# Weight guards issued ahead of the copies of h, w_out's tiles in another order, and other times for loads and spills

## The chip, the core and the metric

One core of a Trainium2 chip runs the whole kernel in one launch. The metric is the device time of an execution in microseconds. The engines are named TensorE (PE in the profile, its weight loads PEld), VectorE (DVE), ScalarE (ACT), GpSimd (POOL) and SyncE (SP, which issues nearly all DMAs).

## The reference

A retention layer without softmax feeds a two-layer network. Per batch entry b (8) and head (8), over 576 positions with 64 channels:

```python
scores = scale * np.matmul(q, k.transpose(0, 1, 3, 2))
Dmat = np.where(rel >= 0, gamma[:, None, None] ** rel[None, :, :], 0.0)
attn = np.matmul(scores * Dmat[None], v)
x = attn.transpose(0, 2, 1, 3).reshape(B * S, H * D)      # 4608 x 512
h = x @ w_in                                              # 512 x 2048
out = (h - np.tanh(h)) @ w_out                            # 2048 x 512
```

All arrays are float32 but the two weight matrices, which come as 64-bit floats.

## The kernel before

**Tiling.** The 576 positions are cut into 9 chunks of 64. A chunk with all 8 batch entries is one block of 512 tokens, and the network runs block by block: `mm1(n, f)` makes tile f (of 16) of h for block n, 12 matmuls of 128x128 by 128x512; `mm2(n, f)` multiplies tile f of h - tanh(h) by w_out's tile f into four output tiles, also 12 matmuls. Each operand is held as a high and a low word, and three products are summed. The retention runs chunk by chunk with a carried state; `entry(p)` handles pair p of batch entries: the output of pair p, the scores of pair p + 1 and the state update, interleaved on TensorE. VectorE then multiplies the scores by a mask into `pm` (L263), ScalarE and VectorE make the two words of x (L278, L280).

**Weights.** w_in and w_out come in 16 tiles each, numbered 0 to 31 in the order `stream` (w_in's 0 to 15, then w_out's in the order `turn`). A tile is loaded raw (`load_w`, 512 KB), and a unit of conversion turns it into two words in the same place: a *guard* on ScalarE (L95 tanh and L98 abs, which make a mask in a buffer of the tag `cv`), three instructions on VectorE (L105, L110, L112), the high word on ScalarE (L117), and the low word on VectorE (L124), which is issued by the next unit's first step. `step()` advances a unit by a third.

**The order of work.** Every engine follows the order in which the program issues its instructions. The first loop over `seq` has 32 iterations, k = 0 to 31: `mm1(0, f)` for k below 16, then `mm1(1, f)`, with entries 4 to 7 after k = 5, 8, 10 and 14. An iteration does one step, `mm1`, then two more steps (one from k = 24 on, none for the last two iterations). Unit u = k + 2 is converted in iteration k. ScalarE's order in an iteration is: copy of h(k) out of its PSUM bank, guard of unit u + 1, high word of unit u; the guard sits in the unit's second step, after mm1. Four banks take h in turn. Then come the loads: `upto("load", k + 7)` issues all tiles with an index below k + 7 (k + 6 from k = 11 on), and `behind` makes each wait for the latest copy of h.

**Places and spills.** h of block 0 and 1 can't be used before w_out is there. Most copies go to memory at once (`g`, spilled by SyncE at L341). Ten tiles of block 0 first stay in places of w_out's tiles (`home`) and are spilled later, place 7, 13, 12, 11 and 10 at k = 16 to 20. Other places of w_out hold early data too: pairs 6 and 7 in 0 to 3, the first chunk's keys in 4 and 5, a table in 6, the first chunk's inputs in 8 to 15. Pair 16 is loaded in halves at k = 9 and 10, pair 17 at k = 14; GpSimd scales their v (L186), and pair 17's q (L185).

**After the loop**, a loop over `late` fetches the spilled tiles one by one (`fetch`), takes tanh and difference (`resume`, L368 and L369), splits them (`words`, L375 and L376) and runs mm2 on them; what is left of the units is done in its first iterations. Blocks 2 to 8 follow with mm1 and mm2 in alternation.

Of the kernel before, what the change touches and what calls it, by code (L numbers as in the profile page):

```python
# [9 lines left out]
F32 = mybir.dt.float32  # L10
F32R = mybir.dt.float32r
I32 = mybir.dt.int32
BF16 = mybir.dt.bfloat16
AF = mybir.ActivationFunctionType
ALU = mybir.AluOpType
PSUM = bass.MemoryType.PSUM

B, H, S, D = 8, 8, 576, 64
NT, DM, DF = B * S, H * D, 2048
P = 128  # L20
NF = DF // P
NCC = DM // P
C = 64
NC = S // C
BLK = B * C
# [33 lines left out]
def behind(tc, name):  # L59

    tc.add_manual_dep(
        tc.nc.cur_bb.bb.instructions[-1], name,
        mybir.DependencyInfo(mybir.DependencyClass.Sync, mybir.DependencyReason.DATA), reason="paced",
    )
# [3 lines left out]
def retention_ffn(ctx: ExitStack, tc: tile.TileContext, ins, out, spill):  # L68
# [4 lines left out]
    pool = ctx.enter_context(tc.tile_pool(name="pool", bufs=2))  # L73
# [3 lines left out]
    mask = const.tile([P, C], F32, name="mask")  # L77
# [3 lines left out]
    win, wout, wraw, masks = {}, {}, {}, {}  # L81
# [9 lines left out]
    def guard(t, f, begin=False):  # L91

        if (t, f) not in masks:
            masks[t, f] = pool.tile([P, DM], I32, tag="cv", bufs=3, name=f"m{t}{f}")
            nc.scalar.activation(masks[t, f], wraw[t, f][:, :, 1].bitcast(F32), AF.Tanh, scale=STEP)  # L95
            if begin:
                return
        nc.scalar.activation(masks[t, f], masks[t, f], AF.Abs, scale=HI_BITS)  # L98

    def unit(k):  # L100

        t, f = stream[k]
        hw, lw = wraw[t, f][:, :, 1], wraw[t, f][:, :, 0]
        z = masks.pop((t, f))
        nc.vector.scalar_tensor_tensor(z, hw, 3, z, op0=ALU.logical_shift_left, op1=ALU.bitwise_and)  # L105
        finish()
        yield
        if 0 < k and k + 1 < at_["load"]:
            upto("guard", k + 2)
        nc.vector.scalar_tensor_tensor(z, lw, 29, z, op0=ALU.logical_shift_right, op1=ALU.bitwise_or)  # L110
        yield
        nc.vector.scalar_tensor_tensor(z, hw, -0x40000000, z, op0=ALU.bitwise_and, op1=ALU.bitwise_or)  # L112
        if k == 0:
            yield
        del wraw[t, f]
        w = const.tile([P, 2, DM], F32R, tag=f"w{t}{f}", name=f"w{t}{f}")
        nc.scalar.copy(w[:, 0], z.bitcast(F32))  # L117
        (wout if t == "o" else win)[f] = w if t == "o" else w.rearrange("p s (c m) -> p s c m", m=P)
        last.append((w, z))

    def finish():
        while last:
            w, z = last.pop()
            nc.vector.tensor_tensor(w[:, 1], z.bitcast(F32), w[:, 0].bitcast(F32), op=ALU.subtract)  # L124


    turn = [NF - 2, NF - 1] + list(range(NF - 2))
    stream = [("i", f) for f in range(NF)] + [("o", f) for f in turn]
    at_ = {"load": 0, "guard": 0, "convert": 0}
    last, going, pace = [], [], []  # L130

    def upto(what, n):
        while at_[what] < min(n, 2 * NF):
            {"load": load_w, "guard": guard}[what](*stream[at_[what]])
            at_[what] += 1
# [17 lines left out]
    loaded, scored, xs, qtabs = {}, {}, {}, {}  # L153

    def load_qtab(c):
        if c not in qtabs:
            if c == 1:
                qtabs[c] = const.tile([P, 4, C], F32, tag="wo6", name="qtab1")
            else:
                qtabs[c] = pool.tile([P, 4, C], F32, tag="qtab", bufs=1, name=f"qtab{c}")  # L160
            nc.sync.dma_start(qtabs[c], qtab_d[c - 1])

    def load_pair(p, u=None):

        if p >= NP:
            return
        c, pr = divmod(p, B // 2)
        load_qtab(c)
        a = loaded["pair", p] if u == 1 else pool.tile([P, 2, 4, 4, C], F32, tag="a", name=f"a{p}")
        if u is None:  # L170
            nc.sync.dma_start(a, qkv_d[c - 1, 2 * pr : 2 * pr + 2].rearrange("u p t i s -> p u t i s"))
        else:
            nc.sync.dma_start(a[:, u], qkv_d[c - 1, 2 * pr + u])
        loaded[2 * p], loaded[2 * p + 1] = a[:, 0], a[:, 1]
        loaded["pair", p] = a
        loaded["qv", p] = a[:, :, 0], a[:, :, 2]

    def prep(p, q=True):
        if p >= NP:
# [12 lines left out]
    def load_early(p):  # L192
        c, pr = divmod(p, B // 2)
        if pr < 2:
            return load_pair(p)
        src = qkv_d[c - 1, 2 * pr : 2 * pr + 2].rearrange("u p t i s -> p u t i s")
        parts = []
        for t in range(2):
            parts.append(const.tile([P, 2, 2, 4, C], F32, tag=f"wo{2 * (pr - 2) + t}", name=f"a_early{p}_{t}"))
            nc.sync.dma_start(parts[t], src[:, :, 2 * t : 2 * t + 2])  # L200
            behind(tc, pace[-1])
        for u in range(2):
            loaded[2 * p + u] = Parts([part[:, u] for part in parts])
        loaded["qv", p] = parts[0][:, :, 0], parts[1][:, :, 0]

    def scale_q(p):
        q, table = loaded["qv", p][0], qtabs[p // (B // 2)]
# [7 lines left out]
    def half(k):  # L215
        return slice(64 * k, 64 * k + 64)
# [38 lines left out]
    def after_score(j, sc, n):  # L255

        if j < B:

            pm = pool.tile([P, 2, 4, C], F32, tag="gh", name=f"pm{j}")
            nc.vector.tensor_tensor(pm[:, 0], sc[:, 0], decay, op=ALU.mult)  # L260
        else:
            pm = pool.tile([P, 2, 4, C], F32, tag="pm", bufs=1, name=f"pm{j}")
            nc.vector.tensor_tensor(  # L263
                pm[:, :n].rearrange("p u i q -> p (u i) q"), sc.rearrange("p u i q -> p (u i) q"),
                mask.unsqueeze(1).broadcast_to([P, 4 * n, C]), op=ALU.mult,
            )
        for u in range(n):
            scored[j + u] = pm[:, u]
# [49 lines left out]
    home = {0: 7, 1: 7, 6: 13, 7: 13, 8: 12, 9: 12, 11: 11, 12: 11, 13: 10, 14: 10}  # L318
# [45 lines left out]

    def resume(n, f):
        g = fetched[n, f]
        th = pool.tile([P, BLK], F32, tag="cv", bufs=3, name=f"th{n}_{f}")
        nc.scalar.activation(th, g, AF.Tanh)  # L368
        nc.vector.tensor_tensor(g, g, th, op=ALU.subtract)  # L369

# [29 lines left out]
    def store(n, t):  # L400
        o = ops[n][t]
        if n == 1:

            if t == 0:
                obs[n] = pool.tile([P, 4, DM], F32, tag="xl", name=f"ob{n}")
            ob = obs[n][:, t]
        else:
            ob = pool.tile([P, DM], F32, tag="cv", bufs=3, name=f"ob{n}_{t}")
        if t % 2 == 0:
            nc.scalar.copy(ob, o)  # L410
        else:
            nc.vector.tensor_copy(ob, o)  # L412
        for u in range(2):
            nc.sync.dma_start(out[2 * t + u, n * C : (n + 1) * C], ob[half(u)])
# [110 lines left out]
    seq = [(n, f) for n in range(2) for f in range(NF)]  # L525
    late = [(1, f) for f in turn] + [(0, f) for f in range(NF)]
    early = {5: 4, 8: 5, 10: 6, 14: 7}
    scales = {2: 4, 4: 5, 7: 6, 9: 7, 13: 8}
    for k, (n, f) in enumerate(seq):
        last_two = k - (len(seq) - 2)  # L530
        if k in (2, 7):
            scale_k(k // 4)
        if k + 1 in early:
            scale_v(early[k + 1])
        if last_two < 0:
            step()
        else:
            fetch(*late[2 + last_two])
        mm1(n, f, ("h", "o2", "h", "o3")[k % 4] if k < len(seq) - 4 else ("o2", "o3", "h", "h")[k % 4])
        if last_two < 0:  # L540
            step()
            if k < 24:
                step()
        if k in scales:
            scale_q(scales[k])
        upto("load", k + (7 if k < 11 else 6))
        if k in (2, 5):
            load_early(B // 2 + 2 + (k - 2) // 3)
        if k in (9, 10):
            load_pair(B, k - 9)  # L550
        for f in [f for f in home if home[f] == (7, 13, 12, 11, 10)[k - NF]] if NF <= k < NF + 5 else []:
            nc.sync.dma_start(spill[0, f], homes[home[f]][:, (f + 1) % 2 if f > 1 else f])
        if k == 3:
            nc.sync.dma_start(krows[1], krows_d[1])
            behind(tc, pace[-1])
            sc = scores_of(B // 2 - 1)
            ms, done = first_states(0, "new")
            run(m_score(B, sc[:, 0]) + m_score(B + 1, sc[:, 1]) + ms, [])
            after_score(B, sc, 2)
            done()  # L560
        if k in early:
            p = early[k]
            more = first_states(2 * (p - 3), f"o{(p + 1) % 2}") if p < B - 1 else None
            entry(p, scores_of(p), more)
        if k == 14:
            load_pair(B + 1)
        if k in (26, 28):
            prep(B + (k - 26) // 2, k == 28)
    p = B
# [16 lines left out]
    for n in range(2, NC):  # L586
        for f in range(NF):
            mm1(n, f)
            if n + 1 < NC and f % 4 == 1:

                sc = psp.tile([P, 2, 4, C], F32, tag="h", bufs=2, name=f"s{n}_{f}")
# [62 lines left out]
```

## Time and profile before

| what | value |
|---|---|
| three runs, median (lowest to highest) | 890.47 us (888.77 to 890.8) |
| profiled execution, its time | 891.8 us |
| profiled execution, its span | 890.0 us |
| mean granted TensorE clock | 0.995 |
| DMA moved | 82.06 MB |

The span runs from the first to the last instruction of the profiled execution; its time has 1.8 us more. All times below are microseconds from the start of the span. In a timeline the first number is the start, the second the length, and a bracket gives the idle time before the instruction and what ended it.

### The profile page before, as it was taken

The page shows a single profiled execution, that of the slowest core. Times are in us where ns is not written, and L with a number is a line of the kernel's source. Part 1 is how long each engine was busy: PE and PEld are TensorE (multiplying, and loading weights), DVE is VectorE, ACT ScalarE, POOL GpSimd, SP SyncE. Part 2 cuts the span into 40 slices and gives each one's busy share as a digit, 9 for nine tenths or more (in the row PEclk, how much of TensorE's full clock was granted, in tenths as well). Part 3 has the DMA queues.
Part 4 walks back from the last instruction along what each step waited for, and adds up shares of the span by engine and source line. Part 5 has one row for each costly group of instructions (what it writes and reads, how often), then busy time and mean ns, then how long its engine had stood idle before and what let it go on. Part 6 is the DMA issues. An engine that isn't in the chain of part 4 may idle for free.

```text
span 890.0 us, 17595 instructions
## 1 busy us (share of the span) xinstructions
PE 877.6 (99%) x7848; PEld 724.3 (81%) x7848; DVE 363.3 (41%) x548; ACT 287.7 (32%) x503; POOL 67.7 (8%) x59
## 2 busy tenths in 40 slices
PE   7999999999999999999999999999999999999997
PEld 6777878788888888888888888888888888888886
DVE  6879777653432332333233233323323322222222
ACT  4887774443222222222222222222222221222222
POOL 0001001210111110111111111111000111000000
PEclk8999999999999999999999999999999999999999
DMA  9966965551311131102111131113111201002001
GB/s 354 325 231 212 342 193 171 167 167 48 96 54 49 48 96 49 54 30 68 47 54 49 49 95 54 49 48 96 49 54 47 62 35 48 1 1 49 1 1 47
DMA packets 31372, 82.06 MB, mean 92 GB/s; under 512 B 3776, under 2 KB 4928, under 8 KB 31296
## 3 DMA queue, kind: packets, MB, share of 16 engines
q1 hardware_dynamic: 30768, 80.02, 27.8%
q8 instruction: 61, 1.00, 0.5%
q10 hardware_dynamic: 528, 0.92, 0.3%
q14 instruction: 15, 0.12, 0.0%
HBM read 63.62 MB, written 17.30 MB: 91 GB/s over the span
## 4 chain that ended last, share of the span: by engine, by line
PE 90%; DMA 3%; DVE 3%; ACT 2%; issue 0%; SPq 0%; DVEq 0%
PE o L393 44%; PE h L327 38%; PE s L252 3%; DMA rwo<-in_w_out_dram 2%; PE new L252 2%; PE own L252 2%; DMA rwi<-in_w_in_dram 1%; DVE mo L110 0%; DVE mo L112 0%; ACT mi L95 0%; ACT mi L98 0%; PE new_first L252 0%; DVE mi L105 0%; DVE wi L124 0%; ACT wi L117 0%
## 5 line engine op out<-in xcount | busy, mean ns | idle before, releaser
L327 PE MATMUL h<-xh,wi 128*128 128x512 f32 x1152 | 307.0, 392 | 2.7 <-ACT g L339 0.8
L393 PE MATMUL o<-wo,gh 128*128 128x512 f32 x1144 | 291.6, 393 | 0.4 <-DVE ob L412 0.4
L327 PEld LDWEIGHTS h<-xh,wi 128*128 128x128 f32 x1152 | 216.3, 189 | 49.7 <-ACT g L339 1.3
L393 PEld LDWEIGHTS o<-wo,gh 128*128 128x128 f32 x1144 | 212.3, 188 | 46.8 <-DVE ob L412 1.5
L354 DVE TENSOR_TENSOR g<-h,g 128x512 f32<-128x512 f32 x114 | 78.8, 691 | 367.1 <-ACT g L353 367.1
L353 ACT ACTIVATE g<-h 128x512 f32<-128x512 f32 x114 | 68.3, 599 | 420.9 <-PE h L327 420.1
L393 PE MATMUL o<-wo,gl 128*128 128x512 f32 x572 | 157.3, 389 | 0.0
L327 PE MATMUL h<-xl,wi 128*128 128x512 f32 x576 | 154.5, 390 | 0.0
L327 PEld LDWEIGHTS h<-xl,wi 128*128 128x128 f32 x576 | 108.7, 189 | 22.9
L393 PEld LDWEIGHTS o<-wo,gl 128*128 128x128 f32 x572 | 107.4, 188 | 22.3
L356 DVE TENSOR_TENSOR gl<-g,gh 128x512 fp32r<-128x512 f32 x113 | 81.0, 717 | 77.5 <-ACT gh L355 70.0
L355 ACT CAST gh<-g 128x512 fp32r<-128x512 f32 x113 | 70.1, 620 | 86.2 <-DVE g L354 86.2
L185 POOL TENSOR_TENSOR a<-a,qtab 128x512 f32<-128x512 f32 x27 | 36.3, 1344 | 605.7 <-DMA a<-in_qkv_dram 547.3
L252 PE MATMUL own<-a,state 64*64 64x64 f32 x960 | 58.9, 221 | 0.0
L252 PE MATMUL own<-pm,a 64*64 64x64 f32 x960 | 57.5, 218 | 0.0
L252 PEld LDWEIGHTS own<-a,state 64*64 64x64 f32 x960 | 47.8, 134 | 0.4 <-issue 0.4
L252 PEld LDWEIGHTS own<-pm,a 64*64 64x64 f32 x960 | 48.0, 135 | 0.0
L252 PEld LDWEIGHTS s<-a 64*64 64x64 f32 x960 | 30.3, 134 | 10.6 <-issue 10.2
L186 POOL TENSOR_TENSOR a<-a,vtab 128x512 f32<-128x512 f32 x28 | 32.2, 1152 | 67.4 <-DVE mi L112 67.4
L252 PE MATMUL s<-a 64*64 64x64 f32 x960 | 34.4, 221 | 0.0
L376 DVE TENSOR_TENSOR gl<-s,gh 128x512 fp32r<-128x512 f32 x30 | 21.6, 720 | 31.2 <-PE o L393 24.4
L375 ACT CAST gh<-s 128x512 fp32r<-128x512 f32 x30 | 18.6, 621 | 39.0 <-PE o L393 27.4
(67 smaller groups left out, 465.0 us busy)
## 6 DMA issues: line engine op xcount, KB each, us to landing
a<-in_qkv_dram SPq DMA_DIRECT2D x29, 1024.0 KB, 5.2
out_dram<-ob SPq DMA_DIRECT2D x69, 128.0 KB, 2.4
rwi<-in_w_in_dram SPq DMA_DIRECT2D x16, 512.0 KB, 5.8
rwo<-in_w_out_dram SPq DMA_DIRECT2D x16, 512.0 KB, 5.1
s<-spill_dram SPq DMA_DIRECT2D x30, 256.0 KB, 2.7
spill_dram<-g SPq DMA_DIRECT2D x20, 256.0 KB, 5.2
a<-in_first_dram SPq DMA_DIRECT2D x7, 384.0 KB, 5.0
spill_dram<-home SPq DMA_DIRECT2D x10, 256.0 KB, 6.3
```

The lines of the kernel that those rows point to most:

```text
L185: nc.gpsimd.tensor_tensor(a[:, :, 0], a[:, :, 0], table, op=ALU.mult)
L186: nc.gpsimd.tensor_tensor(a[:, :, 2], a[:, :, 2], vtab[:, c].unsqueeze(1).unsqueeze(3).broadcast_to([P, 2, 4, D]), op=ALU.mult)
L252: nc.tensor.matmul(out_, w, x, start=start, stop=stop)
L327: nc.tensor.matmul(hp, win[f][:, a, cc, :], x[:, cc, :], start=(k == 0), stop=(k == 3 * NCC - 1))
L353: nc.scalar.activation(g, h, AF.Tanh)
L354: nc.vector.tensor_tensor(g, h, g, op=ALU.subtract)
L355: nc.scalar.copy(gh, g)
L356: nc.vector.tensor_tensor(gl, g, gh.bitcast(F32), op=ALU.subtract)
L375: nc.scalar.copy(gh, g)
L376: nc.vector.tensor_tensor(gl, g, gh.bitcast(F32), op=ALU.subtract)
L393: nc.tensor.matmul(ops[n][t], g[:, t * P : (t + 1) * P], wout[f_][:, a, :], start=(f_ == first and k == 0), stop=(f_ == final and k == 2),)
```

## The change

Guards: a unit's first step now issues the guards of later units, up to unit u + 1 while u is below 5 and up to u + 2 from 5 on, as far as they are loaded; so ScalarE's order in an iteration becomes guard, copy of h(k), high word. The tag `cv` has four buffers instead of three; the room is taken from `pm`, which has no buffer any more: masked scores are written over the pair's k columns. `turn` becomes 14, 15, 8, 9, 4, 5, 6, 0, 1, 2, 3, 7, 13, 12, 11, 10. Loads follow a table `ahead` (as before up to k = 9, then 16, 18, 20, 21, 22, 23, and k + 8 from k = 16 on), home places are spilled at k = 12 (7), 13 (13), 14 (12), 16 (11) and 18 (10). Pair 16's second half is loaded at k = 11, pair 17 at k = 20; pair 7's q is scaled at k = 8 instead of 9 and the second half of the first chunk's keys at k = 6 instead of 7. The second step after mm1 stops at k = 22 instead of 24.

```diff
--- before.py
+++ after.py
@@ -91,7 +91,7 @@
     def guard(t, f, begin=False):
 
         if (t, f) not in masks:
-            masks[t, f] = pool.tile([P, DM], I32, tag="cv", bufs=3, name=f"m{t}{f}")
+            masks[t, f] = pool.tile([P, DM], I32, tag="cv", bufs=4, name=f"m{t}{f}")
             nc.scalar.activation(masks[t, f], wraw[t, f][:, :, 1].bitcast(F32), AF.Tanh, scale=STEP)
             if begin:
                 return
@@ -104,9 +104,12 @@
         z = masks.pop((t, f))
         nc.vector.scalar_tensor_tensor(z, hw, 3, z, op0=ALU.logical_shift_left, op1=ALU.bitwise_and)
         finish()
+        if k > 1:
+
+            upto("guard", min(k + (2 if k < 5 else 3), at_["load"]))
         yield
-        if 0 < k and k + 1 < at_["load"]:
-            upto("guard", k + 2)
+        if k == 1:
+            upto("guard", 3)
         nc.vector.scalar_tensor_tensor(z, lw, 29, z, op0=ALU.logical_shift_right, op1=ALU.bitwise_or)
         yield
         nc.vector.scalar_tensor_tensor(z, hw, -0x40000000, z, op0=ALU.bitwise_and, op1=ALU.bitwise_or)
@@ -124,7 +127,8 @@
             nc.vector.tensor_tensor(w[:, 1], z.bitcast(F32), w[:, 0].bitcast(F32), op=ALU.subtract)
 
 
-    turn = [NF - 2, NF - 1] + list(range(NF - 2))
+
+    turn = [14, 15, 8, 9, 4, 5, 6, 0, 1, 2, 3, 7, 13, 12, 11, 10]
     stream = [("i", f) for f in range(NF)] + [("o", f) for f in turn]
     at_ = {"load": 0, "guard": 0, "convert": 0}
     last, going, pace = [], [], []
@@ -173,7 +177,7 @@
             nc.sync.dma_start(a[:, u], qkv_d[c - 1, 2 * pr + u])
         loaded[2 * p], loaded[2 * p + 1] = a[:, 0], a[:, 1]
         loaded["pair", p] = a
-        loaded["qv", p] = a[:, :, 0], a[:, :, 2]
+        loaded["qk", p], loaded["qv", p] = a, (a[:, :, 0], a[:, :, 2])
 
     def prep(p, q=True):
         if p >= NP:
@@ -201,7 +205,7 @@
             behind(tc, pace[-1])
         for u in range(2):
             loaded[2 * p + u] = Parts([part[:, u] for part in parts])
-        loaded["qv", p] = parts[0][:, :, 0], parts[1][:, :, 0]
+        loaded["qk", p], loaded["qv", p] = parts[0], (parts[0][:, :, 0], parts[1][:, :, 0])
 
     def scale_q(p):
         q, table = loaded["qv", p][0], qtabs[p // (B // 2)]
@@ -259,10 +263,10 @@
             pm = pool.tile([P, 2, 4, C], F32, tag="gh", name=f"pm{j}")
             nc.vector.tensor_tensor(pm[:, 0], sc[:, 0], decay, op=ALU.mult)
         else:
-            pm = pool.tile([P, 2, 4, C], F32, tag="pm", bufs=1, name=f"pm{j}")
+
+            pm = loaded["qk", j // 2][:, :, 1]
             nc.vector.tensor_tensor(
-                pm[:, :n].rearrange("p u i q -> p (u i) q"), sc.rearrange("p u i q -> p (u i) q"),
-                mask.unsqueeze(1).broadcast_to([P, 4 * n, C]), op=ALU.mult,
+                pm, sc, mask.unsqueeze(1).unsqueeze(1).broadcast_to([P, 2, 4, C]), op=ALU.mult,
             )
         for u in range(n):
             scored[j + u] = pm[:, u]
@@ -364,7 +368,7 @@
 
     def resume(n, f):
         g = fetched[n, f]
-        th = pool.tile([P, BLK], F32, tag="cv", bufs=3, name=f"th{n}_{f}")
+        th = pool.tile([P, BLK], F32, tag="cv", bufs=4, name=f"th{n}_{f}")
         nc.scalar.activation(th, g, AF.Tanh)
         nc.vector.tensor_tensor(g, g, th, op=ALU.subtract)
 
@@ -405,7 +409,7 @@
                 obs[n] = pool.tile([P, 4, DM], F32, tag="xl", name=f"ob{n}")
             ob = obs[n][:, t]
         else:
-            ob = pool.tile([P, DM], F32, tag="cv", bufs=3, name=f"ob{n}_{t}")
+            ob = pool.tile([P, DM], F32, tag="cv", bufs=4, name=f"ob{n}_{t}")
         if t % 2 == 0:
             nc.scalar.copy(ob, o)
         else:
@@ -525,10 +529,13 @@
     seq = [(n, f) for n in range(2) for f in range(NF)]
     late = [(1, f) for f in turn] + [(0, f) for f in range(NF)]
     early = {5: 4, 8: 5, 10: 6, 14: 7}
-    scales = {2: 4, 4: 5, 7: 6, 9: 7, 13: 8}
+    scales = {2: 4, 4: 5, 7: 6, 8: 7, 13: 8}
+
+    ahead = {**{k: k + 7 for k in range(10)}, 10: 16, 11: 18, 12: 20, 13: 21, 14: 22, 15: 23}
+    leave = {12: 7, 13: 13, 14: 12, 16: 11, 18: 10}
     for k, (n, f) in enumerate(seq):
         last_two = k - (len(seq) - 2)
-        if k in (2, 7):
+        if k in (2, 6):
             scale_k(k // 4)
         if k + 1 in early:
             scale_v(early[k + 1])
@@ -539,16 +546,16 @@
         mm1(n, f, ("h", "o2", "h", "o3")[k % 4] if k < len(seq) - 4 else ("o2", "o3", "h", "h")[k % 4])
         if last_two < 0:
             step()
-            if k < 24:
+            if k < 22:
                 step()
         if k in scales:
             scale_q(scales[k])
-        upto("load", k + (7 if k < 11 else 6))
+        upto("load", ahead.get(k, k + 8))
         if k in (2, 5):
             load_early(B // 2 + 2 + (k - 2) // 3)
-        if k in (9, 10):
-            load_pair(B, k - 9)
-        for f in [f for f in home if home[f] == (7, 13, 12, 11, 10)[k - NF]] if NF <= k < NF + 5 else []:
+        if k in (9, 11):
+            load_pair(B, (k - 9) // 2)
+        for f in [f for f in home if home[f] == leave.get(k)]:
             nc.sync.dma_start(spill[0, f], homes[home[f]][:, (f + 1) % 2 if f > 1 else f])
         if k == 3:
             nc.sync.dma_start(krows[1], krows_d[1])
@@ -562,7 +569,7 @@
             p = early[k]
             more = first_states(2 * (p - 3), f"o{(p + 1) % 2}") if p < B - 1 else None
             entry(p, scores_of(p), more)
-        if k == 14:
+        if k == 20:
             load_pair(B + 1)
         if k in (26, 28):
             prep(B + (k - 26) // 2, k == 28)
```

## Rows read from the trace of the kernel before

**Rows 1.** The page: TensorE's busy time, and its busy tenths in 40 slices.
```profile
PE 877.6 (99%) x7848; PEld 724.3 (81%) x7848; DVE 363.3 (41%) x548; ACT 287.7 (32%) x503; POOL 67.7 (8%) x59
...
PE   7999999999999999999999999999999999999997
```

**Rows 2.** What TensorE waited for: total us, times, longest us.
```profile
PE s_first L252 <- DMA a<-in_first_dram: 2.8, 4, 1.4
...
PE s L252 <- ACT wi L117: 0.8, 1, 0.8
```

**Rows 3.** Windows: length, busy us of each engine, clock, DMA share, GB/s.
```profile
16.96:190.00 173.04, 169.95 (x1814) 138.80 (x1815) 134.17 (x202) 110.57 (x204) 13.32 (x9) 0.99 0.71 238
190.00:890.00 700.00, 695.30 (x5740) 575.44 (x5738) 220.71 (x327) 169.79 (x284) 54.14 (x46) 1.00 0.17 50
```

**Rows 4.** Timeline of TensorE around its stops.
```profile
44.48 1.20 PE L327 MATMUL h<-xh,wi 128*128 128x512 f32 x4 [0.80 <-issue]
...
58.19 1.19 PE L327 MATMUL h<-xh,wi 128*128 128x512 f32 x4
60.17 0.27 PE L252 MATMUL s<-a_early 64*64 64x64 f32 x2 [0.78 <-ACT wi L117]
...
72.03 0.96 PE L327 MATMUL h<-xh,wi 128*128 128x512 f32 x3 [0.43 <-ACT wi L117]
...
111.60 1.07 PE L327 MATMUL h<-xh,wi 128*128 128x512 f32 x4
113.52 1.20 PE L327 MATMUL h<-xh,wi 128*128 128x512 f32 x4 [0.85 <-ACT g L339]
...
130.05 2.11 PE L393 MATMUL o<-wo,gh 128*128 128x512 f32 x8
```

**Rows 5.** Timeline of VectorE.
```profile
59.38 0.68 DVE L208 TENSOR_TENSOR a_early<-a_early,qtab 128x512 f32<-128x512 f32 x1
...
68.04 1.35 DVE L105 SCALAR_TENSOR_TENSOR mi<-rwi,mi 128x512 int32<-128x512 int32 x1 [0.44 <-ACT mi L98]
...
127.42 0.68 DVE L369 TENSOR_TENSOR s<-s,th 128x512 f32<-128x512 f32 x1
128.03 0.69 DVE L105 SCALAR_TENSOR_TENSOR mo<-rwo,mo 128x512 int32<-128x512 int32 x1
```

**Rows 6.** Timeline of ScalarE.
```profile
38.05 0.58 ACT L339 COPY g<-h 128x512 f32<-128x512 f32 x1 [0.25 <-PE h L327]
...
45.01 0.59 ACT L333 COPY home<-h 128x512 f32<-128x512 f32 x1 [3.42 <-PE h L327]
...
66.18 0.59 ACT L333 COPY home<-h 128x512 f32<-128x512 f32 x1 [1.95 <-PE h L327]
66.66 0.68 ACT L95 ACTIVATE mi<-rwi 128x512 int32<-128x512 f32 x1
...
67.91 0.60 ACT L117 CAST wi<-mi 128x512 fp32r<-128x512 f32 x1
...
129.39 0.60 ACT L375 CAST gh<-s 128x512 fp32r<-128x512 f32 x1
```

**Rows 7.** An issue at 32.15; issues near 32, 73, 94, 61 us: us to landing.
```profile
32.15 0.59 SPq L86 DMA_DIRECT2D rwi<-in_w_in_dram  x1
...
rwi<-in_w_in_dram SPq DMA_DIRECT2D x1, 512.0 KB, 8.4
...
rwo<-in_w_out_dram SPq DMA_DIRECT2D x1, 512.0 KB, 3.5
...
rwo<-in_w_out_dram SPq DMA_DIRECT2D x1, 512.0 KB, 7.7
...
a<-in_qkv_dram SPq DMA_DIRECT2D x1, 512.0 KB, 6.1
```

**Rows 8.** Timeline of GpSimd.
```profile
67.80 1.04 POOL L186 TENSOR_TENSOR a<-a,vtab 128x512 f32<-128x512 f32 x1 [67.36 <-DVE mi L112]
```

**Rows 9.** What ScalarE waited for from 30 to 130 us: total us, times, longest us.
```profile
ACT mo L95 <- DMA rwo<-in_w_out_dram: 5.4, 5, 2.1
```

## The prediction

> **What bounds the kernel now.** I read the page first: TensorE is busy for nearly the whole span [rows 1], so time can only be won where it stands still. The list of what TensorE waited for has the first loads on top and then single waits, none that repeats [rows 2]. The windows then say where room is: up to 190 us its busy time falls 3.1 us short of the window, the DMA engines are 71% busy and VectorE and ScalarE are both loaded; from 190 us on the DMA share is 17% and the slices of the page show TensorE full but for the last one [rows 1, 3]. All that the diff touches runs before about 150 us, except where a masked score is kept, which I come to. So this is a question of a handful of stalls between iteration 6 and the start of the late loop, and the reader should see how small the stake is.
>
> **What each stall costs.** After a stop, four matmuls show 1.20 us and eight 2.11 [rows 4]: one more every (2.11 - 1.20) / 4 = 0.23 us. Four without a stop show 1.07. So the next group is due 4 x 0.23 = 0.91 after such a group starts, 0.16 before its shown end, and a stop costs its idle time + 0.16 + 0.13 for the slow restart, less when another kind of matmul follows. The stop at 113.52, idle 0.85, costs 1.1; at 72.03, idle 0.43, 0.7; at 60.17, idle 0.78, 0.85 (the attention block would have started 0.1 late anyway). The stop at 44.48, idle 0.80, has no releaser ("issue"), and I expect nothing of it. The three that the diff can reach are worth 1.1 + 0.7 + 0.85 = 2.65 us, 0.3% of the time. A 0.2% bound, 1.8 us, about what a measurement of this kernel can tell from no change, needs two thirds of that. What does the new order charge for them?
>
> **Entry(6), the wait at 60.17.** VectorE's scaling of pair 7's q (L208) ends at 60.06 [rows 5]; the timeline names ScalarE's high word of unit 11 [rows 4]. The first moves an iteration earlier (`scales` 9 to 8), the second loses the guard ahead of it (1.25 us on ScalarE, 66.66 to 67.91 [rows 6]). Gain 0.85, bounds 0 and 0.85; I take it whole.
>
> **Guards ahead of the copies of h: what they wait for.** ScalarE runs its program in order, so a guard placed ahead of the copy of h(k) holds that copy, and behind it the high word of unit k+2 that mm1(k+2) needs, until the guard's raw tile has landed. From unit 5 on the guard is for unit u+2 = k+4. The load table for k up to 9 is as before: iteration k issues index k+6, behind its copy of h. So the tile that iteration k+2 guards ahead of its copy was issued after copy k: the lead falls from about three copies to under two.
>
> The tightest case is index 9, issued at 32.15 and landed 8.4 us later, at 40.5, with the queue full [rows 7]; the spill and the load ahead of it keep that order, so it lands at 40.5 again even when issued a microsecond later. Before, its guard came after the copy at 45.01 and waited for nothing. Now it stands ahead of the copy of h(5), which began at 38.05 [rows 6]. From 40.5: guard 1.25, copy 0.5, then casting entry(4)'s output 1.1 (with unit 7's word), and on VectorE xl, state, L105, L124, L110, L112 at 0.6 to 0.7 each [rows 5], then unit 8's word 0.6: 40.5 + 1.25 + 0.5 + 1.1 + 6 x 0.64 + 0.6 = 47.8 with 0.1 of handovers. The matmul at 44.48 is the last of mm1(6), so mm1(8) is due at 44.48 + 0.23 + 12 x 0.227 = 47.4. Cost 0.45; bounds 0 (landing 0.5 earlier) and 2.3 (landing as late after its issue as before, 1.8 more).
>
> The second case is index 16, w_out's tile 14. `ahead[10]` is 16, so it moves from iteration 10 to 11, behind the copy of h(11), and iteration 12 guards it ahead of the copy of h(12). Before, mm1(14) restarted at 72.03; with 0.85 gone, a slow restart of 0.1 at 58.19 too [rows 4], and 0.45 added, copy 11 moves from 66.18 to about 65.7, and with the 0.6 gone mm1(14) would be due at 70.9. The load is issued at 66.25, when that copy ends. One such load took 3.5 us where nothing else moved and 7.7 in the saturated stretch, a half pair with a load ahead of it 6.1 [rows 7]; here the queue is empty, so I take 4.2, near the first. Landing 70.4, guard 1.25, copy 0.5, word 0.6 and a handover: 72.8, that is 0.8 later than before instead of 1.1 earlier. Bounds 72.1 (3.5 us) and 74.7 (6.1 us): 0.1 to 2.7 lost against before.
>
> The Trainium skill, "DMA: Bandwidth & Descriptors", section "Anatomy of one DMA", gives a fixed 2.0 us plus the bytes over 436 GB/s, for a transfer issued from GpSimd; for 512 KB that is an estimate of 3.2 us, by which mm1(14) would start at 71.8 and the sum would be lower by 1.0. The rows, of SyncE's queue, are all above it, and I go by them.
>
> **Pair 16 and GpSimd.** Its second half moves from k = 10 to k = 11 and stands third behind copy 11; such a transfer took 6.1 us [rows 7], so it lands near 73. GpSimd's scaling of v then falls on unit 15 and the scaling of q that entry(7) needs. When it ran at 67.80, L105 took 1.35 us instead of 0.69 [rows 5, 8]: 0.66 more, of which about 0.3 is covered by the step into entry(7). I take 0.35; bounds 0 and 0.66.
>
> **Loads and spills from k = 12 on, the wait at 113.52.** ScalarE waited five times for w_out's tiles, 5.4 us in all [rows 9], fell behind, and the copy of h(25) came so late that mm1(28), which takes its bank, stopped until 113.52 [rows 4]. The new order of tiles (8, 9, 4, 5 first) and the spills at 12 to 18 start loads one to two iterations earlier; from k = 16 index k+7 is issued and guarded three iterations later, 8 us, where the slowest landing of these tiles was 7.7 [rows 7]. I take the 1.1 as won, bounds 0 and 1.1. The data moved are the same.
>
> **Two steps fewer.** `k < 22` instead of 24 leaves the last two thirds of unit 29 for the late loop. There, L369 ends at 128.1; L110 and L112, one started 0.6 us after L369's start and the next 0.7 on, end near 129.4, unit 29's word 0.6, and only then comes gh for the third mm2: end 130.6, where it was 129.99 with the guard of index 31 ahead of it, and mm2 began at 130.05 with no slack [rows 4, 5, 6]. Cost 0.6; bounds 0, if the two instructions find room before L369, and 1.1, if a second gh tile comes late by as much. **The fourth cv buffer and pm in k's place** cost no instruction: the mask still waits for the scores, and k is not read afterwards. I price it at nothing: the multiplication has the same size and is hidden behind TensorE's next projection, which does not read it; were that cover gone, its length, some 0.7 us like every VectorE instruction here [rows 5], would show at each entry after 190 us, where TensorE stands still nowhere [rows 3].
>
> **The sum**: -0.85, +0.45 and the 0.7 of mm1(14) are all inside "0.8 later than before at mm1(14)"; then +0.35, -1.1, +0.6. Together +0.65 us. The profiled execution took 891.8 with a span of 890.0; its sum is 892.4. The median of the runs is 1.3 below that execution, 890.47, so I predict 891.1.
>
> **Rivals.**
> *The stalls simply go.* The early tile lands as soon as 3.5 us after its issue, the guards find their data, the late loop hides unit 29: -2.65, or 887.8. For it: ScalarE idles 3.4 us before 45.01 and 1.95 before 66.18 [rows 6], so it can afford some waiting; against it: those idle times lie where the guards now wait.
> *The loop closes.* Guard waits for load, copy for guard, next load for copy. If index 9 lands 1.8 us later than I take it, as late after its issue as before, then mm1(8) and all that follows slip by as much: +0.65 + 1.8 = +2.45, or 892.9. It decides from a landing past about 41.6 us, 1.1 late, where the sum passes 1.8. For it: 8.4 us in a full queue; against: the queue, not the issue, sets that landing.
> *DMA stays behind.* Traffic moved into iterations 11 to 16 keeps the queue full, copy 25 is late again: +1.1 on top, 892.2.
>
> **How the numbers follow.** Forecast (890.0 to 892.2) 0.51, first rival 0.26, second 0.15, third 0.08. The first is faster by over 0.2%; the second and half of the third are slower, and a little of the forecast's upper end: faster 0.26, same 0.52, slower 0.22. For 8 in 10 the range reaches well into the first rival and to the second: 888.1 to 893.0; the forecast's own is 890.0 to 892.2.
>
> **What would show it.** Right: the wait at 60 us gone; ScalarE idle before a guard near 38 to 40 and again near 68 to 70 us, ended by the DMA of rwi and rwo; TensorE stopping at mm1(14) for ScalarE's word for 1 to 2 us; no stop near 113; a stop of about 0.6 at the third mm2. The prediction is wrong if index 16 is on chip before 68 us, or if mm1(7) or mm1(8) stops for over a microsecond.

## The result, and the profile after

The change made the kernel slower. In eleven executions each, side by side, the median went from 889.32 us (888.65 to 891.08) to 893.12 (891.31 to 894.99): a ratio of 1.0043, 95% interval 1.0032 to 1.0054, or 3.8 us. The forecast was 891.1 with a range to 893.0; the time lies 0.1 above that range. Of all executions in this document two are left out of the ratios: one of number 12 (1777.29 us, twice the others) and one of before beside numbers 5 to 8 (973.04 us, at a granted clock of 0.85).

The profiled execution of the new kernel took 892.09 us with a span of 890.3. The page's line of engines beside [rows 1]:

```profile
PE 876.3 (98%) x7848; PEld 722.6 (81%) x7848; DVE 363.8 (41%) x548; ACT 288.1 (32%) x503; POOL 67.4 (8%) x59
```

The counts of instructions are those of before: nothing was added, only moved. What TensorE waited for (total us, times, longest us), beside [rows 2]:

```profile
PE h L331 <- ACT wi L120: 2.6, 3, 1.4
PE s_first L256 <- DMA a<-in_first_dram: 2.2, 4, 1.4
PE o L397 <- ACT gh L379: 1.5, 2, 0.8
...
PE s L256 <- PE h L331: 0.5, 1, 0.5
```

ScalarE's high word of a weight tile (L120, L117 before) is now waited for three times, gh (L379, L375 before) twice. The timeline of TensorE has the six places, beside [rows 4]:

```profile
34.52 1.20 PE L331 MATMUL h<-xh,wi 128*128 128x512 f32 x4 [0.50 <-ACT wi L120]
...
46.91 1.20 PE L331 MATMUL h<-xh,wi 128*128 128x512 f32 x4 [0.72 <-ACT wi L120]
...
71.31 1.20 PE L331 MATMUL h<-xh,wi 128*128 128x512 f32 x4 [1.36 <-ACT wi L120]
...
74.85 0.27 PE L256 MATMUL s<-a 64*64 64x64 f32 x2 [0.53 <-PE h L331]
...
129.69 2.11 PE L397 MATMUL o<-wo,gh 128*128 128x512 f32 x8 [0.78 <-ACT gh L379]
...
146.66 2.11 PE L397 MATMUL o<-wo,gh 128*128 128x512 f32 x8 [0.71 <-ACT gh L379]
```

These are mm1(5), mm1(8), mm1(14), entry(7), and the third and the eighth mm2 of the late loop. The stops at 60.17 and 113.52 of [rows 4] are gone. The timeline of ScalarE, beside [rows 6], shows where the first three come from:

```profile
32.12 0.69 ACT L95 ACTIVATE mi<-rwi 128x512 int32<-128x512 f32 x1 [1.19 <-DMA rwi<-in_w_in_dram]
...
39.54 0.68 ACT L95 ACTIVATE mi<-rwi 128x512 int32<-128x512 f32 x1 [1.19 <-DMA rwi<-in_w_in_dram]
...
40.78 0.57 ACT L343 COPY g<-h 128x512 f32<-128x512 f32 x1
...
68.94 0.66 ACT L95 ACTIVATE mo<-rwo 128x512 int32<-128x512 f32 x1 [2.86 <-DMA rwo<-in_w_out_dram]
69.63 0.63 ACT L98 ACTIVATE mo<-mo 128x512 int32<-128x512 int32 x1
70.17 0.57 ACT L337 COPY home<-h 128x512 f32<-128x512 f32 x1
70.64 0.62 ACT L120 CAST wi<-mi 128x512 fp32r<-128x512 f32 x1
```

A guard (L95) stands idle until its raw tile lands; the copy of h and the high word queue up behind it, and TensorE restarts when the word is there: 70.64 + 0.62 = 71.26, restart at 71.31. VectorE's instructions meanwhile take twice as long where GpSimd runs, beside [rows 5, 8]; first VectorE, then GpSimd:

```profile
73.22 1.53 DVE L212 TENSOR_TENSOR a<-a,qtab 128x512 f32<-128x512 f32 x1
...
142.07 0.68 DVE L127 TENSOR_TENSOR wo<-mo,wo 128x512 fp32r<-128x512 f32 x1
142.89 1.56 DVE L380 TENSOR_TENSOR gl<-s,gh 128x512 fp32r<-128x512 f32 x1
144.38 1.52 DVE L373 TENSOR_TENSOR s<-s,th 128x512 f32<-128x512 f32 x1
```

```profile
72.64 1.57 POOL L190 TENSOR_TENSOR a<-a,vtab 128x512 f32<-128x512 f32 x1 [72.19 <-DVE mi L113]
...
142.12 1.79 POOL L189 TENSOR_TENSOR a<-a,qtab 128x512 f32<-128x512 f32 x1 [34.54 <-DMA a<-in_qkv_dram]
143.87 1.49 POOL L190 TENSOR_TENSOR a<-a,vtab 128x512 f32<-128x512 f32 x1
```

At 73.22 the scaling of q that entry(7) needs is stretched. At 142 to 146 a leftover low word of the weights (L127) comes first, then gl of the seventh mm2 and the difference s for the eighth take 1.5 us each instead of 0.69; ScalarE's gh for the eighth starts only at 145.99, and mm2 stops.

**Which execution of before to compare with.** The span of before is 890.0, that of after 890.3, yet the medians differ by 3.8 us. So the unchanged kernel was profiled once more ("before again" below, span 887.2). Windows of 17 to 22 us, of before, of before again and of after, one fence each (us, then each engine's busy time and count, mean granted clock, DMA share, GB/s):

```profile
17.00:22.00 5.00, 5.00 (x13) 3.96 (x14) 4.82 (x8) 1.72 (x3) 0.00 (x0) 0.54 1.04 395
```

```profile
17.00:22.00 5.00, 4.63 (x19) 3.48 (x20) 4.57 (x8) 3.63 (x7) 0.00 (x0) 1.00 1.03 396
```

```profile
17.00:22.00 5.00, 4.53 (x19) 3.42 (x20) 4.50 (x8) 3.62 (x8) 0.00 (x0) 1.00 1.02 385
```

In the first profile of before the granted clock was 0.54 in this stretch and 13 matmuls were made in place of 19. Mm1(5) began 18.17 us after mm1(0), against 16.46 in before again: 1.7 us that no wait accounts for. TensorE's timeline around mm1(28), in before again:

```profile
109.91 1.98 PE L327 MATMUL h<-xh,wi 128*128 128x512 f32 x8
111.73 0.61 PE L327 MATMUL h<-xl,wi 128*128 128x512 f32 x2
```

No idle time stands there: the stop of 113.52 is missing too. What ScalarE waited for from 30 to 130 us in before again, beside [rows 9], is less as well:

```profile
ACT mo L95 <- DMA rwo<-in_w_out_dram: 3.9, 5, 1.0
```

From here on after is set beside before again. Starts of groups on TensorE after mm1(0), which began at 17.27 and 17.34 us:

| start of | before again | after | later by | step |
|---|---|---|---|---|
| mm1(5) | 16.46 | 17.18 | 0.72 | +0.72 |
| mm1(8) | 28.82 | 29.57 | 0.75 | +0.03 |
| mm1(11) | 44.35 | 44.10 | -0.25 | -1.00 |
| mm1(14) | 53.07 | 53.97 | 0.90 | +1.15 |
| mm1(15) | 58.05 | 59.57 | 1.52 | +0.62 |
| mm1(28) | 93.55 | 95.07 | 1.52 | 0 |
| third mm2 | 109.97 | 112.35 | 2.38 | +0.86 |
| eighth mm2 | 126.00 | 129.32 | 3.32 | +0.94 |
| end of span | 869.89 | 872.97 | 3.08 | -0.24 |

The 3.1 us are there, in four places: +1.15 at mm1(14), +0.62 at entry(7), +0.86 and +0.94 in the late loop, with the gain of entry(6) (-1.00) mostly eaten by mm1(5). Each column is one execution; numbers 5 and 6, whose program is after's up to mm1(9), begin mm1(5) at 16.46 and 16.42, so the step there is not in every execution of it.

### The profile page after: what moved, and what is told of

Same layout as the page of the kernel before. It is cut to its first block, busy times and chain, and to the rows that moved or that the text cites. A ratio compares the mean times of both kernels' runs of the same rounds, so it can differ in the third digit from the quotient of the medians.

```text
span 890.3 us, 17598 instructions
## 1 busy us (share of the span) xinstructions
PE 876.3 (98%) x7848; PEld 722.6 (81%) x7848; DVE 363.8 (41%) x548; ACT 288.1 (32%) x503; POOL 67.4 (8%) x59
## 4 chain that ended last, share of the span: by engine, by line
PE 92%; DMA 3%; ACT 2%; DVE 2%; issue 0%; SPq 0%; DVEq 0%; ACTq 0%
PE o L397 44%; PE h L331 41%; PE s L256 3%; DMA rwi<-in_w_in_dram 3%; PE new L256 2%; PE own L256 2%; DMA rwo<-in_w_out_dram 0%; ACT mi L95 0%; ACT wi L120 0%; DVE s L373 0%; ACT mi L98 0%; DVE mi L115 0%; DVE mi L113 0%; PE new_first L256 0%; ACT home L337 0%
## 5 line engine op out<-in xcount | busy, mean ns | idle before, releaser
L256 PE MATMUL own<-a 64*64 64x64 f32 x960 | 57.5, 218 | 0.0
L256 PEld LDWEIGHTS own<-a 64*64 64x64 f32 x960 | 48.0, 135 | 0.0
L379 ACT CAST gh<-s 128x512 fp32r<-128x512 f32 x30 | 18.7, 622 | 39.2 <-PE o L397 28.1
```

The source lines that it names most:

```text
L256: nc.tensor.matmul(out_, w, x, start=start, stop=stop)
L379: nc.scalar.copy(gh, g)
```

## The experiments

**The theory:** a guard ahead of the copy of h turns the landing of a tile into a wait of the copy, and two steps fewer push the leftover of units into the late loop, where two gh tiles come late. **Its rivals:** the other order and times of loads and spills cost the time, by DMA or by pair 16 and GpSimd, and the guards are innocent; or the landing is late by the place in which tile 16 is issued and not by how far ahead the guards run; or the difference is spread between executions. Each time but one is a median of 8 to 12 executions; the ratio is to the kernel before on the same chip, with its 95% interval. The medians of before in these comparisons were 889.47 to 889.95 us.

**1. Before again.** No edit.

> The kernel before once more, for its own trace and for the spread. Ratio 1.000 within 0.001. The profiled execution of before lost about 2.2 us to a lower granted clock between 17 and 22 us; if that differs from execution to execution, this trace may show the head at the full clock, and then ends nearer 888 than 890 us, with the stops near 44, 60, 72 and 113 us in the same places.

Measured: 889.23 us, 0.9995 [0.9986, 1.0004]. The comparison itself adds nothing; its profile is the second column above.

**2. Loads alone.** The new kernel with the guards where they were before, three cv buffers and pm in its own place:

```diff
-        if k > 1:
-
-            upto("guard", min(k + (2 if k < 5 else 3), at_["load"]))
         yield
-        if k == 1:
-            upto("guard", 3)
+        if 0 < k and k + 1 < at_["load"]:
+            upto("guard", k + 2)
```

> The changed kernel with the guards in their old place (after the copy of h), three cv buffers and a pm buffer of its own; loads, spills, order of w_out's tiles and steps are the changed ones. Theory 1 (guards ahead of the copies hold ScalarE until a tile has landed): faster than before, 0.997 to 0.999, since the stops near 60 and 113 us go and no guard stands ahead of a copy; only the two steps fewer cost up to 2 us. Rival (the traffic moved into iterations 11 to 20 and GpSimd's scaling cost it): as slow as the changed kernel, 1.003 to 1.005.

Measured: 890.57 us, 1.0003 [0.9994, 1.0013]. The 0.4% of the change needs the guards (or the buffers that go with them, which number 3 keeps and is no slower), but the gain expected of the rest did not come. VectorE's timeline and the list of what TensorE waited for say why:

```profile
72.21 0.69 DVE L209 TENSOR_TENSOR a<-a,qtab 128x512 f32<-128x512 f32 x1 [1.25 <-DMA a<-in_qkv_dram]
```

```profile
PE o L395 <- ACT gh L377: 1.2, 2, 0.7
...
PE s L253 <- issue: 1.1, 1, 1.1
```

Pair 16's second half, a load later than before, is itself late for entry(7), and TensorE waits 1.2 us for two late gh tiles. In the profile mm1(14) begins 1.96 us earlier than in before again; entry(7) takes 1.07 of this back, and the stretch from the first mm2 to the end costs 1.9.

**3. Guards one ahead.** The new kernel, with guards ahead of the copy but only up to unit u + 1:

```diff
-            upto("guard", min(k + (2 if k < 5 else 3), at_["load"]))
+            upto("guard", min(k + 2, at_["load"]))
```

> The changed kernel, but every unit guards only unit u + 1 in its first step, still ahead of the copy of h. Each guarded tile has then been issued one iteration longer. Theory 1: the stops at mm1(5), mm1(8) and mm1(14), 0.7 + 0.9 + 1.6 us in the trace of the changed kernel, go; those of the late loop, 1.9 us, stay: ratio to before 1.000 to 1.002. Rival (loads, spills, GpSimd): unchanged, 1.003 to 1.005.

Measured: 889.78 us, 0.9998 [0.9988, 1.0009], a little below what was expected. TensorE no longer waits for a high word at all:

```profile
PE o L397 <- ACT gh L379: 1.2, 2, 0.7
...
PE h L331 <- issue: 0.7, 1, 0.7
```

So the place ahead of the copy does no harm. Guarding two units ahead does, with the loads where they are.

**4. Guards alone.** The kernel before with the guards of the change (and four cv buffers and pm in k's place, which they need), with the old loads, spills and steps. One execution.

```diff
+        if k > 1:
+
+            upto("guard", min(k + (2 if k < 5 else 3), at_["load"]))
         yield
-        if 0 < k and k + 1 < at_["load"]:
-            upto("guard", k + 2)
+        if k == 1:
+            upto("guard", 3)
```

> The kernel before with the guards of the change, four cv buffers and pm in the place of k; loads, spills, order and steps as before. From k = 11 on iteration k - 1 issues index k + 4, and iteration k guards it ahead of its copy. Theory 1: the loop closes, copy to load to landing to guard to copy takes 4 to 7 us for a landing and 2 us on ScalarE where an iteration has 2.7: some 3 to 5 us more in each of a dozen iterations, 925 to 945 us. Rival: moving the guards on ScalarE costs no more than a few us, 888 to 895.

Measured: 931.21 us, 41 above before. This is the closed loop in full; what ScalarE waited for, and its timeline:

```profile
ACT mo L95 <- DMA rwo<-in_w_out_dram: 50.9, 15, 4.9
```

```profile
91.70 0.69 ACT L95 ACTIVATE mo<-rwo 128x512 int32<-128x512 f32 x1 [3.74 <-DMA rwo<-in_w_out_dram]
...
92.96 0.57 ACT L341 COPY g<-h 128x512 f32<-128x512 f32 x1
...
98.43 0.66 ACT L95 ACTIVATE mo<-rwo 128x512 int32<-128x512 f32 x1 [4.39 <-DMA rwo<-in_w_out_dram]
...
99.66 0.57 ACT L341 COPY g<-h 128x512 f32<-128x512 f32 x1
...
105.33 0.66 ACT L95 ACTIVATE mo<-rwo 128x512 int32<-128x512 f32 x1 [4.58 <-DMA rwo<-in_w_out_dram]
```

Guard waits for load, copy for guard, the next load for the copy: one turn takes 6.7 and 6.9 us here (98.43 - 91.70, 105.33 - 98.43), where an iteration's 12 matmuls are worth 2.7. What keeps the change out of this is among the parts that are as before here: the load table, the order of the tiles, the spills. Which of them does it was not tried.

**5. Steps to 24.** The new kernel with the old bound of the second step:

```diff
-            if k < 22:
+            if k < 24:
```

> The changed kernel, but the second step after mm1 runs until k = 24 as before, so that unit 29 is done before the late loop. Theory 1 (four terms: guards ahead early, tile 16, GpSimd at entry(7), two steps fewer): the stops of the late loop, 1.05 at the third mm2 and 0.98 at the eighth in the trace of the changed kernel, go; the changed kernel at 1.0035 to 1.0043 falls by 0.0022, to 1.0013 to 1.0022. Rival (the steps are hidden, the late stops come from the spilled tiles in the new order): no change.

Measured: 891.07 us, 1.0015 [1.0005, 1.0025], as expected. Both late gh tiles are off the list:

```profile
PE h L331 <- ACT wi L120: 1.8, 3, 0.9
```

Two steps fewer are worth about 2.5 us of the loss (1.0043 - 1.0015; the trace has 0.86 + 0.94 = 1.8). Each ratio is uncertain by 0.001, so such a difference is uncertain by about 1.3 us.

**6. Tile 16 at 10.** Index 16 is issued in iteration 10, as before:

```diff
-    ahead = {**{k: k + 7 for k in range(10)}, 10: 16, 11: 18, ...
+    ahead = {**{k: k + 7 for k in range(10)}, 10: 17, 11: 18, ...
```

> The changed kernel with index 16 (w_out's tile 14) loaded at k = 10, as before, instead of 11; nothing else. Theory 1: ScalarE finds the tile when it comes to its guard, the idle time of 2.86 us before that guard and the stop of 1.6 us at mm1(14) go; ratio lower by about 0.0018, 1.0018 to 1.0026. Rival (the stop at mm1(14) comes from VectorE's share of the conversion, stretched by GpSimd): the stop only shrinks by a few tenths, 1.003 to 1.004.

Measured: 891.5 us, 1.0017 [1.0007, 1.0028], just below what was expected. The guard of index 16, in ScalarE's timeline, has no idle time ahead of it, and the wait of mm1(14) is gone:

```profile
68.02 0.68 ACT L95 ACTIVATE mo<-rwo 128x512 int32<-128x512 f32 x1
```

```profile
PE h L331 <- ACT wi L120: 0.8, 1, 0.8
```

One number in a table holds about 2.3 us (1.0043 - 1.0017; the trace has 1.15 at mm1(14) and, behind it, a part of entry(7)'s 0.62), as uncertain as in number 5.

**7. Loads one earlier.** The guards stay two ahead, all loads up to k = 10 go one iteration earlier:

```diff
-    ahead = {**{k: k + 7 for k in range(10)}, 10: 16, 11: 18, ...
+    ahead = {**{k: k + 8 for k in range(10)}, 10: 18, 11: 18, ...
```

> The changed kernel with guards two units ahead as they are, but each load up to k = 9 issued one iteration earlier (k + 8 instead of k + 7) and indices 16 and 17 at k = 10. If it is the lead between issue and guard that costs, and not the place of the guards on ScalarE, the stops at mm1(5), mm1(8) and mm1(14) (0.7, 0.9 and 1.6 us) mostly go although every guard stays where it is: 1.0005 to 1.0020. Rival (a guard of 1.25 us ahead of each copy is itself what makes the words late): unchanged within 0.001 of the changed kernel.

Measured: 889.75 us, 0.9997 [0.9988, 1.0006], better than expected. One high word is still waited for, and the gh tiles, which this edit leaves as they are:

```profile
PE o L397 <- ACT gh L379: 1.2, 2, 0.7
...
PE h L331 <- ACT wi L120: 0.5, 1, 0.5
```

Numbers 3 and 7 do the same from two ends, one by asking for a tile later and one by sending for it earlier, and both land at the time of before. What costs is the lead between issue and guard.

**8. One ahead, steps to 24.** Edits 3 and 5 together.

> Guards one unit ahead and steps until k = 24, the rest as changed. Theory 1: what is left of the stops is the one at 44 us without a releaser, 0.2 at entry(7) and the old 0.4 near 175 us; guard_one_ahead stood at 0.9998, and 2.0 us more go: 0.9970 to 0.9985, faster than both kernels. Rival: as guard_one_ahead, 0.999 to 1.001.

Measured: 888.77 us, 0.9989 [0.998, 0.9997]: a gain, but less than expected. A wait that the others covered is now in the open; the list for TensorE and VectorE's timeline:

```profile
PE s L256 <- issue: 1.4, 1, 1.4
PE o L397 <- DVE ob L416: 1.0, 1, 1.0
```

```profile
73.17 0.69 DVE L212 TENSOR_TENSOR a<-a,qtab 128x512 f32<-128x512 f32 x1 [2.76 <-DMA a<-in_qkv_dram]
```

Entry(7) stops for VectorE's scaling of q, and that waits for pair 16's second half, issued in iteration 11 instead of 10, as in number 2. (The "issue" in the list hides it: VectorE's row names the DMA. The wait for ob is one stop at 174 us; in number 9 the list has 0.2 for it.)

**9. One ahead, steps to 24, pair 16 at 10.** Number 8, and pair 16's second half where it was before:

```diff
-        if k in (9, 11):
-            load_pair(B, (k - 9) // 2)
+        if k in (9, 10):
+            load_pair(B, k - 9)
```

> one_ahead_steps_24 with pair 16's second half loaded at k = 10 as before, instead of 11 behind two weight tiles. Theory 1 as it now stands: entry(7) waited there 1.5 us for the scaling of pair 16's q, and VectorE waited 2.76 us for that half to land; both go: 0.9989 falls by 0.0016 to about 0.9973. Rival (the stop is GpSimd stretching VectorE, whenever the half lands): unchanged, 0.9985 to 0.9992.

Measured: 886.89 us, 0.997 [0.9959, 0.9981], as expected: faster than the kernel before, and with it than the change. Of what TensorE waited for, once the warm-up and the first chunk (own_first, near the start) are done, nothing is left over 0.6 us:

```profile
PE own_first L256 <- issue: 1.7, 1, 1.7
...
PE h L331 <- ACT xh L282: 0.6, 1, 0.6
...
PE h L331 <- ACT wi L120: 0.2, 1, 0.2
```

**10. Loads, pair 16 at 10, steps to 24.** Number 2 with the same two repairs, so the guards behind the copy as before. It asks what the guards ahead of the copy are worth when nothing is late.

> loads_alone (guards behind the copies as before, three cv buffers, pm of its own) with pair 16's second half at k = 10 and steps until k = 24. It stood at 1.0003 with stops of 1.25 at entry(7) and 0.7 and 0.9 in the late loop. Theory 1: all three go, 0.9970 to 0.9980, so that guards ahead add nothing to the loads. Rival (guards one unit ahead are worth something by themselves): 0.0010 or more above one_24_pair10.

Measured: 888.31 us, 0.9988 [0.9978, 0.9999]. It lies between before and number 9; the intervals of 9 and 10 overlap by a hair, 0.9978 to 0.9981. By the medians the rival of the expectation holds: guards one ahead seem worth 1.6 us (0.9988 - 0.997). But all eight executions of number 9 had a mean granted clock of 0.999 or more, and only five of number 10's twelve; these five have a median of 887.64, 0.75 above number 9's. In the profiles the stretch from the first mm2 to the end of the span takes 765.77 us here and 765.01 in number 9, and 765.70 in number 8, which has number 9's guards and the stop for ob. So some 0.75 us is left for the guards, and that it is theirs isn't shown.

**11. Scales alone.** The kernel before with two moved scalings and nothing else:

```diff
-    scales = {2: 4, 4: 5, 7: 6, 9: 7, 13: 8}
+    scales = {2: 4, 4: 5, 7: 6, 8: 7, 13: 8}
...
-        if k in (2, 7):
+        if k in (2, 6):
```

> The kernel before with pair 7's q scaled at k = 8 instead of 9 and the keys' second half at k = 6 instead of 7, nothing else. By the prediction's term for entry(6) the stop near 59 us, 0.85 us, goes: 0.9988 to 0.9995. Rival (the stop is ScalarE's high word of unit 11, as the list of waits names it): it stays, 1.000.

Measured: 888.25 us, 0.9981 [0.9971, 0.999], a little more than expected. TensorE waits for no high word any more, at entry(6) or at mm1(14):

```profile
PE h L327 <- issue: 0.6, 2, 0.3
...
PE o L393 <- DVE ob L412: 0.2, 1, 0.2
```

So the wait of 60.17 goes with these two scalings. The keys' scaling is ScalarE's work and the q's is VectorE's, so the run doesn't tell the two apart by itself; by the program entry(6) reads pair 7's q and no weight tile, and the q was ready 0.11 us before it began, so the q is what it hung on, though the timeline put it down to ScalarE's word [rows 4, 5]. Behind it nothing more is won: from mm1(11) to mm1(15) it takes 13.92 us here and 13.71 in before again.

**12. Two ahead, loads earlier, steps to 24, pair 16 at 10.** The guards of the change untouched, with edits 7, 5 and the pair of 9.

> Guards two units ahead as in the changed kernel, with loads one iteration earlier, pair 16's second half at k = 10 and steps until k = 24. loads_one_earlier stood at 0.9997 with stops of 0.7 near 47 us and 0.7 and 0.9 in the late loop. Theory 1 (lead, not place): the late stops go, 0.9975 to 0.9985, within 0.001 of one_24_pair10. Rival (guards two ahead cost by their place): 0.9995 or more.

Measured: 887.34 us, 0.997 [0.996, 0.998], again better than both kernels. Guards two ahead of the copy are harmless once the tiles up to index 17 have a further iteration to land:

```profile
PE h L331 <- issue: 0.8, 2, 0.6
...
PE h L331 <- ACT wi L120: 0.2, 1, 0.2
```

## Why the prediction was wrong

The sign of the sum was right, +0.65 us on the profiled execution, and its size was not. By its own steps:

- **Entry(6), -0.85: right.** Between mm1(8) and mm1(11) after gains 1.00 us on before again, and number 11, with nothing but the two moved scalings, gains 1.12.
- **Index 9 and mm1(8), +0.45: right in kind, too small, 0.75 to 1.14.** The guard at 39.54 waits for the tile, which landed at 39.52 (forecast 40.5). TensorE stops for 0.72 us at mm1(8), which replaces a stop of 0.69 without a releaser that before again has at 42.97: net 0.03. Index 7 does the same two iterations earlier and costs 0.72 at mm1(5); the prediction took index 9 for the tightest case and didn't price this one. Together 0.75 in this execution. The profiles of numbers 5 and 6, the same program up to there, have no stop at mm1(5) and keep the one without a releaser (0.64 and 0.76); mm1(8) begins 0.98 and 1.14 later than in before again. So the stop at mm1(5) is not in every execution, and the cost of index 9 is.
- **Index 16 and mm1(14), net +0.8: right.** The tile was issued at 65.10 and was on chip at 68.92, 3.8 us later (4.2 forecast), and mm1(14) begins 0.90 later than in before again. Number 6 removes this wait by one number. The Trainium skill, "DMA: Bandwidth & Descriptors", section "Anatomy of one DMA", would give an estimate of 3.2 us by its fit for a transfer issued from GpSimd; the row of SyncE's queue stands above it here too.
- **Pair 16 and GpSimd at entry(7), +0.35: right in kind, 0.62.** GpSimd ran from 72.64, and VectorE's scaling of q took 1.53 us, 0.84 above its 0.69; it ended at 74.75, and TensorE went on at 74.85. Assumed were 0.66 more, less a cover of 0.3; in the profiles of numbers 5 and 6, where GpSimd stretched the instruction ahead of it, the term is 0.50 and 0.39. The half's own lateness, seen in numbers 2 and 8 as 1.1 to 1.4 us, is covered in after by the stop at mm1(14).
- **The stop at 113.52, -1.1: this step failed.** The new kernel has no such stop, as forecast, but neither has the old one in its second profile, nor in number 11. It belonged to one execution, whose span is 2.8 us longer than that of before again: 1.7 us by the clock and about 1.1 by this stop, for which ScalarE's waits for w_out's tiles had added up to 5.4 us and not 3.9. The text took the profile for the kernel: it went down by 1.3 to the median of the runs and still counted the stop as won. Without this term the sum is +1.75, which on the median of eleven executions gives 891.1.
- **Two steps fewer, +0.6: the second step that failed, 1.80.** The third mm2 is 0.86 late. The eighth is 0.94 late on top, which stood in the text as a bound (1.1, "if a second gh tile comes late by as much") and was left out of the sum. Number 5 shows both go with the steps. The rows at 142 to 146 have one low word more on VectorE and GpSimd's work on the next pair right behind it. GpSimd works there in number 5 too (141.95 to 145.25) and no mm2 stops, but the last low word there is at 136.93: the leftover of the units is what comes on top.
- **A fourth cv buffer, and pm in k's place, 0:** not tried apart from the guards. Number 3, which has both, is at 0.9998, so they can't cost much.

The signs that the prediction named all came, from ScalarE's idle times at 38 to 40 and 66 to 69 us to the stop of 0.78 at the third mm2. They could not show the first error: no stop near 113 is what the old kernel has too.

With the terms as measured, 0.75 - 1.00 + 1.15 + 0.62 + 0.86 + 0.94 = 3.32, less 0.24 given back by the end: 3.1 us. The ratio says 3.8. Of the 2.4 us between the forecast's 0.65 and this, the stop at 113.52 makes 1.1 and the steps 1.2. The difference of 0.7 to the ratio is not placed in a trace: the median of after's eleven executions lies 1.0 us above its profiled one, that of before again 0.3. It may be the granted clock. After's four executions with a mean clock of 0.999 have a median of 892.42, the four at 0.995 and 0.996 one of 894.60; of the 31 executions of before beside numbers 9 to 12, eighteen at 0.999 or more have 889.31 and five at 0.996 have 891.66. A low clock costs either kernel some 2 us, and after met it in four executions of eleven; for before's eleven it is not on record.

Of the rivals, "The loop closes" is the mechanism of number 4, but in after it is not what adds the time: index 9 landed at 39.5, not later than the 40.5 assumed. "DMA stays behind" is out, since mm1(28) shows no step in the table. "The stalls simply go" is what numbers 9 and 12 reach, and 887.8 was its forecast; they measured 886.89 and 887.34.

## What to carry to other kernels

An instruction that is moved ahead in an engine's order takes its wait with it, and all behind it on that engine then waits too: move the issue of its data by the same distance, or don't move it. Before a stall is counted as won, see that it is in a second profile of the unchanged kernel; a single execution had lost 2.8 us, 1.7 by its clock and 1.1 in a stop, that its repeat had not. A change made of several parts can be a loss as a whole and hold a gain of 0.3%: undo its parts one by one, and look after each for the wait that comes up next.

## What the runs showed of the hardware

- The same kernel had a mean granted TensorE clock of 0.54 from 17 to 22 us in one execution, near the lower of its two levels (1.2 and 2.4 GHz), and of 1.00, the upper one, in another, in a stretch in which all engines do the same program's work. It cost 1.7 us, and the mean over the span was 0.995 against 1.000. Of the fourteen profiles four have less than 0.75 there (before 0.54, number 3 0.50, number 8 0.73, number 10 0.51), and in these mm1(1) begins 3.8 to 5.0 us after mm1(0), in the other ten 3.2. What decides it was not tried.
- VectorE's multiplication or subtraction on two 128x512 f32 tiles took 1.52 to 1.56 us instead of 0.69 while GpSimd ran a multiplication of that size, and GpSimd's own 1.49 to 1.79. The Trainium skill, "GPSIMD Engine Reference", section "8. Key points", says that the two engines contend for their SBUF interfaces when VectorE reads two operands from SBUF; the rows agree. In these three pairs of rows and the one of [rows 5, 8] VectorE's instruction ends 0.54 to 0.55 us after GpSimd's, though it began 0.24 to 0.77 us after it: that reads as work held until GpSimd has ended, not as half speed.
- TensorE stopped for 0.3 to 0.8 us between 42 and 45 us, with no releaser ("issue"), in thirteen of the fourteen profiles, whatever was changed; only the new kernel's, which had stopped at mm1(5), has none. Its cause was not looked for on the chip.
